# Chunked attention with a two-layer MLP behind it on one core: the opening stretch with and without 128 matmuls of the identity

## The chip, the cores and the metric

One core of one Trainium2 chip runs the whole program. The metric is the device time in microseconds (us) of one execution. A profiled execution also has a span, from the first to the last instruction of the program; all places in the profile (us) count from the start of that span.

## The reference

Attention is computed inside chunks of 64 tokens only, for 8 batches, 8 heads, 576 tokens and a head dimension of 64; its output, 4608 tokens by 512, goes through two matrix products with a leaky ReLU between them.

```python
# q, k, v: [8, 8, 576, 64]; w_in: [512, 2048]; w_out: [2048, 512]
scores = scale * np.matmul(q_c, k_c.transpose(0, 1, 2, 4, 3))   # chunks of 64
scores = scores - np.max(scores, axis=-1, keepdims=True)
attn = np.exp(scores)
attn = attn / (np.sum(attn, axis=-1, keepdims=True) + 1e-09)
out = np.matmul(attn, v_c)
x = out.transpose(0, 2, 1, 3).reshape(4608, 512)
h = x @ w_in
g = np.maximum(0.01 * h, h)
return g @ w_out
```

## The kernel before, in words

**Units and blocks.** The attention works on 36 units of 128 tokens (two chunks, all eight heads). The MLP works on blocks of 128, 256 or 512 tokens (`BLOCKS`, line 46). All matmuls are in 16 bits, but for the transposes of the first unit, whose q and k come in 32 bits by a DMA each from SyncE and ScalarE (lines 121 to 124).

**Stages of a unit u.** Each is a small function, and the text names it by its letter:
- `tq`, `tk` (line 259): four transposes of q, of k, on TensorE into PSUM (`qp`, `kp`, one buffer each).
- `q` (lines 272, 274): two copies of `qp` into the block-diagonal tile `QZ`, on ScalarE where the name ends in .1, else on VectorE. `k` (lines 279, 281): the copy of `kp` to `KT`.
- `s` (line 309): eight matmuls of 64 columns, the scores, into PSUM `Sp` (one buffer).
- `m`, `b` (VectorE, lines 318, 322): row maximum, and the difference. `x` (ScalarE, line 328): the exponential. `z` (VectorE, lines 334 to 338): sum, plus 1e-9, reciprocal. `n` (VectorE, line 343): the product.
- `e` (line 351): four transposes of the probabilities on TensorE into `tpe`; `c` (line 358 on ScalarE, 360 on VectorE): the copy to `et`.
- `v` (line 376): eight matmuls of 64 columns with the values (`VB`) into `xp`. `tpe` and `xp` share a single PSUM buffer (tag `ox`), so `e` of a unit waits until `a` of the unit before it is done.
- `a` (ScalarE, line 389): the copy of `xp` into `xT`, the MLP's input.

**The MLP.** `A j.a` (line 157) is one group of sixteen 128-column matmuls of the first layer for the 128-token block j, from quarter a of `w_in`; `G j.a` (line 172, ScalarE) its leaky ReLU. `B j.p` (line 182) is four 512-column matmuls of the second layer; `O j` (line 193) copies a finished block out, and a DMA stores it. The first-layer and second-layer results, and the tile of the filler, share four PSUM buffers (tag `mm`).

**What sets the order.** Every engine executes its instructions in program order. For the first six units that order is a string written out by hand, `FRONT` (line 430), which names the stages one after another; the loop from line 473 on follows for the other units. In `FRONT` stand also `y` (VectorE memsets of `QZ` and `VB`), `w` (the same on ScalarE), `I` (the identity copied to 32 bits on ScalarE, line 410, which the first `tq` and `tk` use), and `i` followed by a number: that many filler matmuls, `idle`. Their result is read by nobody:

```python
def idle(n):
    t = psp.tile([128, 4, 128], FP32, name="idle", tag="mm", bufs=4)
    for i in range(n):
        nc.tensor.matmul(out=t[:, i % 4, :], lhsT=ident, rhs=ident, start=True, stop=True)
```

`FRONT` calls it nine times: i12, i4, i23, i55, i7, i3, i3, i12 and i9, together 128 matmuls of 128 columns, each with its weight load. The nine calls are all in the part ahead of `A0.0`, the first group of the MLP.

**Loads.** GpSimd issues the DMAs of q, k, v and the weights in the order of `LOADS` (line 133); the identity is made there after the first of them (line 140).

Of the kernel before, what the change touches and what calls it, by code (L numbers as in the profile page):

```python
# [16 lines left out]
def kernel(  # L17
# [401 lines left out]
    def zero_act(i):  # L419
# [8 lines left out]
            )  # L428

    FRONT = (  # L430
        "y0 y1 y2 y4 w3 I y5 i12 tq0 tk0 q0.1.1 q0.0 tq1 k0.1 q1.0.1 i4 s0 tk1 m0 k1 b0 q1.1.1 i23 s1 x0 "
        "m1 b1 z0 x1 z1 i55 tq2 q2.0.1 n0 i7 tk2 k2 q2.1 i3 e0 n1 c0.1 s2 m2 i3 v0 a0 b2 i12 e1 x2 c1 i9 "
        "v1 z2 A0.0 a1 A1.0 n2 G0.0 e2 A0.1 c2 v2 tq3 a2 A1.1 q3.1 G0.1 q3.0 tk3 A2.0 G1.0 k3.1 G1.1 s3 "
        "A0.2 G2.0 m3 A1.2 b3 x3 A2.1 G0.2 z3 A0.3 G1.2 tq4 G2.1 n3 A1.3 G0.3 e3 G1.3 A2.2 c3 q4.0.1 v3 "
        "tk4 a3 A2.3 k4.1 q4.1 A3.1 y6 G2.3 G2.2 A3.0 G3.1 s4 A3.3 m4 A3.2 b4 G3.3 G3.0 B0.1 G3.2 B3.1 x4 "
# [104 lines left out]
```

## Time and profile before

| | us |
|---|---|
| device time, median of 3 runs | 294.11 (294.11 to 294.14) |
| device time of the profiled execution | 294.1 |
| its span | 292.3 |
| TensorE busy | 284.4 |
| VectorE busy | 182.7 |
| ScalarE busy | 152.5 |
| filler matmuls (line 396) | 9.6 busy, 128 instructions, from 3.8 to 18.1 |
| first matmul of the MLP (line 157) | at 18.57 |

The 1.8 us between the device time and the span lie outside the program's own instructions. In a timeline row the first number is the start, the second the time from the first instruction's start to the last one's end; matmuls are pipelined, so one of them is shown with 219 ns or more although a row of them starts one every 56 ns. In the chain of waits the second number is only the time by which a piece carried the chain on, so there the time of n matmuls divided by n is their pace.

### The profile page before, as it was taken

To read this page: it belongs to the slowest core of one execution; us is meant where nothing else is said; L and a number is where in the kernel's file an instruction comes from. 1 tells how busy PE (TensorE), PEld (TensorE's weight loads), DVE (VectorE), ACT (ScalarE), POOL (GpSimd) and SP (SyncE) were. 2 spreads that over 40 slices of the span, in tenths; PEclk is the share of its full clock that TensorE was granted. 3 is DMA by queue.
4 is the path that set the end of the run, shared out by engine and by line. 5 is a ranking of instruction groups with operands and counts; after the bars stand their busy time and mean duration, and the time that the engine had idled before them with its cause. 6 is when DMAs were issued, how large, how long until landed. Compare 5 with 4: busy or idle time off the path is not lost.

```text
span 292.3 us, 6210 instructions
## 1 busy us (share of the span) xinstructions
PE 284.4 (97%) x2556; PEld 181.8 (62%) x2556; DVE 182.7 (63%) x338; ACT 152.5 (52%) x270; POOL 119.4 (41%) x148
## 2 busy tenths in 40 slices
PE   4999999999999999999999999999999999999995
PEld 3989955878677766767676754444454444444444
DVE  5776536879899898888877888787777720000000
ACT  5457713756456545646454547733763387127511
POOL 8857547898509837920394379210000000000000
PEclk9999999999999999999999999999999999999999
DMA  9999999999999999999499999992111320120022
GB/s 131 162 193 194 202 157 184 168 144 146 127 126 61 148 147 135 139 132 99 66 135 138 105 85 148 94 137 90 56 23 31 112 69 0 38 88 21 0 74 72
DMA packets 192332, 32.00 MB, mean 109 GB/s; under 512 B 183472, under 2 KB 187824, under 8 KB 192304
## 3 DMA queue, kind: packets, MB, share of 16 engines
q0 software_dynamic: 170208, 18.10, 114.0%
q1 hardware_dynamic: 21056, 13.24, 19.4%
q8 instruction: 20, 0.33, 0.4%
q10 hardware_dynamic: 1040, 0.26, 0.4%
q14 instruction: 8, 0.07, 0.1%
HBM read 36.70 MB, written 9.44 MB: 158 GB/s over the span
## 4 chain that ended last, share of the span: by engine, by line
PE 97%; POOL 1%; ACT 1%; issue 1%; DVE 0%; POOLq 0%
PE hT L157 43%; PE oP L182 41%; PE Sp L309 3%; PE xp L376 3%; PE idle L396 3%; PE oP L203 1%; PE qp L259 1%; PE tpe L351 1%; PE kp L259 1%; POOL k_in L69 0%; DVE QZ L274 0%; ACT KT L281 0%; ACT QZ L272 0%; POOL q_in L69 0%; ACT osb L211 0%
## 5 line engine op out<-in xcount | busy, mean ns | idle before, releaser
L157 PE MATMUL hT<-xT,w_inT 128*128 128x128 f16 (+2 forms) x1152 | 134.3, 273 | 0.0
L182 PE MATMUL oP<-w_outT,gT 128*128 128x512 f16 x560 | 128.2, 379 | 0.0
L157 PEld LDWEIGHTS <-w_inT 128*128 128x128 f16 x1152 | 90.0, 98 | 32.7
L172 ACT ACTIVATE gT<-hT 128x512 f16<-128x512 f32 x144 | 83.8, 597 | 32.5 <-PE hT L157 32.3
L182 PEld LDWEIGHTS <-gT 128*128 128x128 f16 x560 | 52.3, 98 | 56.3
L193 ACT ACTIVATE osb<-oP 128x512 f32<-128x512 f32 x35 | 20.9, 596 | 64.6 <-PE oP L182 62.7
L87 POOL DMA_DIRECT2D q_d<-in_q_dram x48 | 38.7, 818 | 35.3 <-DVE QZ L291 31.6
L318 DVE TENSOR_REDUCE mx<-Sp 128x8 f32<-128x512 f32 x36 | 24.9, 691 | 31.0 <-PE Sp L309 30.8
L87 POOL DMA_DIRECT2D k_d<-in_k_dram x48 | 38.7, 817 | 2.1 <-DMA q_d<-in_q_dram 1.1
L291 DVE STREAM_TRANSPOSE QZ<-q_d 64x512 f16<-64x512 f16 (+1 forms) x60 | 38.2, 644 | 0.4
L389 ACT ACTIVATE xT<-xp 128x512 f16<-128x512 f32 x36 | 21.4, 594 | 20.6 <-PE xp L376 20.6
L96 POOL DMA_DIRECT2D VB<-in_v_dram x16 | 18.4, 1159 | 20.8 <-PE xp L376 20.5
L334 DVE TENSOR_REDUCE z<-ex 128x8 f32<-128x512 f16 x36 | 23.6, 654 | 4.7 <-ACT ex L328 4.6
L322 DVE TENSOR_TENSOR sh<-Sp,mx 128x512 f32<-128x512 f32 x36 | 24.9, 691 | 1.2
L343 DVE TENSOR_TENSOR en<-ex,zi 128x512 f16<-128x512 f16 x36 | 24.8, 690 | 1.2
L328 ACT ACTIVATE ex<-sh 128x512 f16<-128x512 f32 x36 | 22.6, 628 | 5.3 <-DVE sh L322 5.3
L299 DVE STREAM_TRANSPOSE KT<-k_d 128x512 f16<-128x512 f16 (+1 forms) x30 | 19.4, 654 | 0.8
L376 PEld LDWEIGHTS <-VB 128*128 128x128 f16 x288 | 13.1, 98 | 5.6
L309 PEld LDWEIGHTS <-QZ 128*128 128x128 f16 x288 | 13.2, 99 | 5.4 <-DVE QZ L274 0.2
L309 PE MATMUL Sp<-KT,QZ 128*128 128x64 f16 x288 | 14.5, 195 | 0.1
L376 PE MATMUL xp<-et,VB 128*128 128x64 f16 x288 | 14.3, 193 | 0.0
L396 PE MATMUL idle<-ident 128*128 128x128 f16 x128 | 9.6, 233 | 3.8 <-POOL ident masks.py:199 3.8
(42 smaller groups left out, 104.2 us busy)
## 6 DMA issues: line engine op xcount, KB each, us to landing
out_dram<-osb SPq DMA_DIRECT2D x35, 256.0 KB, 2.3
VB<-in_v_dram POOLq DMA_DIRECT2D x16, 288.0 KB, 6.0
q_d<-in_q_dram POOLq DMA_DIRECT2D x48, 72.0 KB, 6.0
k_d<-in_k_dram POOLq DMA_DIRECT2D x48, 72.0 KB, 5.3
w_inT<-in_moe_w_in_dram POOLq DMA_DIRECT2D x8, 256.0 KB, 9.2
w_outT<-in_moe_w_out_dram POOLq DMA_DIRECT2D x4, 512.0 KB, 9.5
q_in<-in_q_dram POOLq DMA_DIRECT2D x7, 128.0 KB, 9.7
k_in<-in_k_dram POOLq DMA_DIRECT2D x7, 128.0 KB, 9.0
```

The source lines that it names most:

```text
L87: nc.gpsimd.dma_start(out=t[p0:p0 + 32, m, :, :, :].rearrange("p h b d -> p (h b) d"), in_=src[b, h0:h0 + 2, :, dh * 32:dh * 32 + 32].rear ...
L157: nc.tensor.matmul(out=hT[:, i, :], lhsT=w_inT[:, t, fc * 128:(fc + 1) * 128], rhs=xT[:, t, r0:r0 + tb], start=(t == 0), stop=(t == NT - 1),)
L172: nc.scalar.activation(out=gT[j][:, nf * a:nf * a + nf, :], in_=HT.pop((j, a)), func=AFT.Prelu, bias=0.0, scale=1.0, alpha=0.01)
L182: nc.tensor.matmul(out=o, lhsT=gT[j][:, fc, ti * 128:(ti + 1) * 128], rhs=w_outT[:, fc, :], start=(n == 0 and fc == part * 4), stop=(n == ...
L291: nc.vector.transpose(out=qz[s * CH:(s + 1) * CH, :, e0:e0 + n, s, :], in_=qkd[b][0][s * CH:(s + 1) * CH, :, at:at + n * CH].rearrange("p ...
L309: nc.tensor.matmul(out=Sp[:, i, :], lhsT=qz[:, 2 * m + g, e, :, :], rhs=kt[:, 2 * m + g, e, :], start=True, stop=True)
L318: nc.vector.tensor_reduce(out=MX[u], in_=SP[u], axis=AXL.X, op=ALU.max)
L322: nc.vector.tensor_tensor(out=SH[u], in0=SP.pop(u), in1=MX.pop(u).unsqueeze(2).to_broadcast((128, 8, CH)), op=ALU.subtract)
L328: nc.scalar.activation(out=E[u], in_=SH.pop(u), func=AFT.Exp, bias=0.0, scale=SCL)
L334: nc.vector.tensor_reduce(out=z, in_=E[u], axis=AXL.X, op=ALU.add)
L343: nc.vector.tensor_tensor(out=E[u], in0=ex, in1=ZI.pop(u).unsqueeze(2).to_broadcast((128, 8, CH)), op=ALU.mult)
L376: nc.tensor.matmul(out=xp[:, t, e, :], lhsT=VB[b % NVB][:, t, c, :], rhs=et[:, t // 2, e, t % 2, :] if u < UD else et[:, t % 2, e, t // 2, :],
```

## The change

The nine `i` entries are taken out of `FRONT`. All other entries stand in the same order, and the loads, tiles and loops are the same. `idle` stays defined and is not called.

```diff
     FRONT = (
-        "y0 y1 y2 y4 w3 I y5 i12 tq0 tk0 q0.1.1 q0.0 tq1 k0.1 q1.0.1 i4 s0 tk1 m0 k1 b0 q1.1.1 i23 s1 x0 "
-        "m1 b1 z0 x1 z1 i55 tq2 q2.0.1 n0 i7 tk2 k2 q2.1 i3 e0 n1 c0.1 s2 m2 i3 v0 a0 b2 i12 e1 x2 c1 i9 "
+        "y0 y1 y2 y4 w3 I y5 tq0 tk0 q0.1.1 q0.0 tq1 k0.1 q1.0.1 s0 tk1 m0 k1 b0 q1.1.1 s1 x0 "
+        "m1 b1 z0 x1 z1 tq2 q2.0.1 n0 tk2 k2 q2.1 e0 n1 c0.1 s2 m2 v0 a0 b2 e1 x2 c1 "
         "v1 z2 A0.0 a1 A1.0 n2 G0.0 e2 A0.1 c2 v2 tq3 a2 A1.1 q3.1 G0.1 q3.0 tk3 A2.0 G1.0 k3.1 G1.1 s3 "
...
```

## The prediction

> **What bounds the kernel now.** I read the page first: busy times, the 40 slices, the shares of the chain, and the group of the filler.
>
> ```profile
> PE 284.4 (97%) x2556; PEld 181.8 (62%) x2556; DVE 182.7 (63%) x338; ACT 152.5 (52%) x270; POOL 119.4 (41%) x148
> PE   4999999999999999999999999999999999999995
> PEclk9999999999999999999999999999999999999999
> L396 PE MATMUL idle<-ident 128*128 128x128 f16 x128 | 9.6, 233 | 3.8 <-POOL ident masks.py:199 3.8
> ```
>
> TensorE is busy from the first slice to the last. The list of what TensorE waited for, asked from 18.6 us to the end, has no row, and the only hole that the single instructions show there is 0.17 us ahead of e2, the transposes at 20.52. So whatever moves the start of A0.0 (18.57), or slows TensorE behind it, moves the end by as much, less those 0.17 us. The page's chain gives the filler 2.8% of the span; whether that time can be had back is decided by what each run of filler stands in front of. The chain in order of time shows TensorE's pace too:
>
> ```profile
> 8.20 0.43 PE idle L396 x4
> 8.63 0.43 PE Sp L309 x8
> 9.06 0.43 PE kp L259 x4
> 9.48 1.39 PE idle L396 x23
> 10.87 0.31 PE Sp L309 x8
> 11.18 3.07 PE idle L396 x55
> ...
> 18.34 0.39 PE xp L376 x8
> 18.73 1.79 PE hT L157 x32
> ```
>
> Four filler matmuls take 0.43 us at 8.2 (107 ns each) and 55 take 3.07 us at 11.2 (55.8 each): the same instruction runs at half pace up to about 9.6 us, and at full pace from there. (23 at 55.8 would be 1.28 us, the row has 1.39: two were still slow.) The page's clock row and its windows say full clock even before that, so there I go by the pace. That the clock is also taken away, the stretches behind the last matmul (end 288.9) show; the columns are the length, the busy time of PE, PEld, DVE, ACT and POOL, the granted clock, the DMA share and GB/s:
>
> ```profile
> 289.50:292.80 3.30, 0.00 (x0) 0.00 (x0) 0.00 (x0) 0.00 (x0) 0.00 (x0) 1.00 0.12 40
> 292.90:294.30 1.40, 0.00 (x0) 0.00 (x0) 0.00 (x0) 0.00 (x0) 0.00 (x0) 0.50 0.00 0
> ```
>
> The clock held through 3.9 us without a matmul and was half by 4.0. Last the timeline of the chain's end, to see what the filler covers:
>
> ```profile
> 15.28 0.40 PE L351 MATMUL tpe<-ident,en 128*128 128x128 f16 x4
> 15.71 0.60 ACT L358 ACTIVATE et<-tpe 128x512 f16<-128x512 f16 x1
> 16.36 0.39 PE L376 MATMUL xp<-et,VB 128*128 128x64 f16 x8
> 16.79 0.60 ACT L389 ACTIVATE xT<-xp 128x512 f16<-128x512 f32 x1 [0.48 <-PE xp L376]
> 17.44 0.38 PE L351 MATMUL tpe<-ident,en 128*128 128x128 f16 x4
> 17.86 0.42 DVE L360 COPY et<-tpe 128x512 f16<-128x512 f16 x1
> 18.34 0.39 PE L376 MATMUL xp<-et,VB 128*128 128x64 f16 x8
> ```
>
> e0, c0, v0, a0, e1, c1, v1 follow each other at 0.04 to 0.06 us, each the moment that the one before has ended. They alternate between TensorE and another engine, and the filler (i3, i12, i9) lies in between.
>
> **The change, run by run.** i12 (3.80 to 5.05): tq0 starts at 5.11, and its 32-bit identity is ready at 5.05 (ScalarE, 4.76 + 0.29). Nothing gained. i4: k0 ends on VectorE at 8.165 and s0 could start 0.05 later, at 8.22; it starts at 8.42, behind i4. That is the one place where filler delays: **-0.20**. i23: s1 starts at 10.78, q1 on ScalarE ends at 10.72. Covered. i55 and i7: tq2 and tk2 could go at 12.17 and 13.28 (their loads land at 12.12 and 13.23) instead of 14.09 and 14.71. But their copies stand in program order behind x1 on ScalarE and behind n0 on VectorE, and e0 waits for n0 (end 15.22), which ends an unbroken VectorE run from m1 (11.22) on. Nothing gained. i3, i3, i12, i9: the chain just shown. The nine filler tiles also leave the four `mm` buffers; nothing waited for these in the front. The loads come by GpSimd, which waits for no filler; w_in's first quarter has landed at 16.22, the second at 18.95, both early enough.
>
> So with an unchanged clock the whole change is worth 0.20 us. The cost is the clock. Without filler TensorE has, after the unchanged tq0 and tk0 (5.11 to 7.08), tq1, s0 and tk1 between 7.62 and 9.08, then s1 at 10.6, tq2 at 12.2, tk2 at 13.3, e0 at 15.3, s2 at 15.8 and v0 at 16.6, each 0.2 to 0.45 us of issue. In before, 3.1 us of unbroken work (3.80 to 6.87) had not raised the clock, and it rose only after another 1.95 us (7.62 to 9.57). I take the slow clock to last through the front.
>
> (1) *The chain at the slow clock.* Per step, slow row minus fast row: s1 like s0, 0.64 for 0.41: +0.23. e0 like tk1 (0.61) for 0.40: +0.21. v0 like s0, 0.64 for 0.39: +0.25 and the same for e1, 0.61 for 0.38: +0.23. v1 up to the issue of A0.0, 0.45 (s0 to tk1, 8.42 to 8.87) for 0.23: +0.22. Together 1.14; s2 slows too but ends as n1 does on VectorE, at 16.4. With i4's -0.20 A0.0 starts **+0.94** later, at 19.5. Bounds: -0.20 if all is fast, +0.94 if all is slow; I take the latter, as the slow rows are nearest to work in short bursts.
>
> (2) *The dense run until the clock rises.* From 19.5 TensorE has unbroken work at 107 instead of 55.8 ns per 128 columns, so each slow us loses 0.48. How long it lasts no row shows for such a run; the nearest two are 1.95 us (from the end of the pause to the rise) and 5.77 (from the first matmul to the rise). That makes 0.93 to 2.75; between two ends that are equally far I take the middle, 3.86 us: **+1.84**.
>
> (3) *Given back.* The hole ahead of e2: **-0.17**. n2 ends 0.45 later (c1 holds VectorE), at 20.9; e2 is reached only at 22.9.
>
> Sum: 0.94 + 1.84 - 0.17 = +2.61. The profiled execution had 294.1, as the median; so **296.7**, a span of 294.9. With (2) at its ends: 295.8 to 297.6.
>
> The Trainium skill, "TensorE: Matmul & The Clock Gate", "What's actually happening", says that activity is judged in free-running windows of 3.413 us. This trace agrees: rise (9.57) to fall (between 292.8 and 292.9) is 83.0 of them. By that rule the window edges here are 9.57, 19.81 and 23.22, the dense run is slow for 3.7 us, and the sum is 296.6.
>
> **Rivals.** *A, the clock rises at 9.6 anyway and holds.* Place: tq1, s0 and tk1, 1.26 us of issue where before has 1.95 unbroken. If that suffices, or if the rise comes with time and not with work, and if the bursts behind it hold the clock, nothing is left but i4: 294.1 - 0.2 = 293.9, not slower. It decides from the rise alone, as no later pause (at most 1.7 us, tk2 to e0) comes near the 3.9 us that the clock survived at the end. Against it: the 3.1 us that were not enough. The same page ("Why this matters for your kernels") asks only that no pause exceeds some 3 us; that rule would give this rival's time, and no row of the front can test it. A rise at 9.6 that is lost again before 19 would give 296.5, and counts with the forecast.
>
> *B, the front's bursts count.* The clock is up at A0.0 or under 1.95 us after it: 294.1 + 0.94 - 0.17 + (0 to 0.93) = 294.9 to 295.8. For it: v0, e1, v1 come close together. Against: they are still mostly pauses.
>
> *C, it takes longer than 5.77 us*, because the dense run starts just after a stretch judged idle: beyond 297.6, 0.48 per us, to about 298.5 with two more. Against: nothing interrupts the run.
>
> *D, the chain's 2.8% is simply saved*: 294.1 - 8.2 = 285.9. Against it stands the whole run-by-run list.
>
> **How the numbers follow.** Forecast 0.70, A 0.10, B 0.08, C 0.10, D 0.02. The forecast's own range is 295.8 to 297.6; taking in nearly all of B and the nearer half of C, 295.0 to 298.0 holds 0.82. About 0.2% (0.6 us) is what a measurement of this kernel can tell from no change. Faster: D and a little more, 0.03. Same: A, 0.11. Slower: 0.86.
>
> **What would show it.** Tk1 at 8.66, s1 at 10.56 with 53 ns between its matmuls (29 refutes step 1), n0 at 14.6 as before, A0.0 at 19.5, first-layer matmuls 107 ns apart up to 21.5 to 25.3 and 56 from there, no wait of TensorE behind it, and the same distance from that rise to the end. The forecast is wrong if s1 and v0 run at 29 ns, or if some copy or DMA that now has slack turns up ahead of A0.0.

## The result and the profile after

The kernel without the filler takes 296.52 us in the median of 4 runs (295.95 to 297.52), the one with it 294.12 (294.11 to 294.14): ratio 1.0093, 95% interval 1.008 to 1.0106, so 2.4 us slower. The profiled execution took 296.64 us with a span of 294.8.

The page of the kernel after, the lines that answer to those of before:

```profile
PE 280.0 (95%) x2428; PEld 176.7 (60%) x2428; DVE 184.0 (62%) x338; ACT 152.4 (52%) x270; POOL 119.4 (40%) x148
PE   2479999999999999999999999999999999999995
PEclk9999999999999999999999999999999999999999
```

TensorE has 4.4 us less to do and ends 2.5 us later. The first two slices now show its pauses. The clock row is the same and shows nothing of what follows. The chain of waits of the kernel after, in order of time (start, how long the piece carried the chain, what):

```profile
10.52 0.62 PE Sp L309 x8
...
15.22 0.62 PE tpe L351 x4
...
15.86 0.61 ACT et L358
...
16.51 0.60 PE xp L376 x8
...
17.13 0.61 ACT xT L389
...
17.78 0.60 PE tpe L351 x4
...
18.40 0.44 DVE et L360
...
18.88 0.58 PE xp L376 x8
19.46 3.41 PE hT L157 x32
22.88 0.27 PE tpe L351 x4
23.15 0.39 PE hT L157 x7
```

Two things are to be seen. Each burst of TensorE in the alternating chain takes about 0.6 us, against 0.4 in before; the copies between them take what they took. And the first 32 matmuls of the MLP take 3.41 us, 107 ns each, where before has 1.79 us for 32; the seven behind e2 are at 56 again. The clock came up at about 22.9, in the middle of e2. A0.0 starts at 19.28 (18.57 in before).

The one new hole of TensorE behind that is ahead of e3. The timeline of the kernel after (start, length, engine, operation) leads back to an addition on VectorE:

```profile
28.17 2.33 POOL L96 DMA_DIRECT2D VB<-in_v_dram  x2
...
29.68 0.82 DVE L336 TENSOR_SCALAR ze<-z 128x8 f32<-128x8 f32 x1
...
30.45 0.93 POOL L69 DMA_DIRECT2D q_in<-in_q_dram  x1
...
31.52 0.23 PEld L351 LDWEIGHTS <-en 128*128 128x128 f16 x4 [0.26 <-DVE en L343]
```

The same addition in before:

```profile
27.44 0.20 DVE L336 TENSOR_SCALAR ze<-z 128x8 f32<-128x8 f32 x1
...
28.49 2.33 POOL L96 DMA_DIRECT2D VB<-in_v_dram  x2
```

The addition `ze` on eight numbers per row takes 0.82 us, where the median is 0.17. It stands beside GpSimd's issue of the loads of v; in before it fell ahead of these. n3 and e3 come later by that, and TensorE has a hole of 0.25 us. Why the addition takes longer there was not tried.

### The profile page after: what moved, and what is told of

Same layout as the page of the kernel before. It is cut to its first block, busy times and chain, and to the rows that moved or that the text cites. A ratio compares the mean times of both kernels' runs of the same rounds, so it can differ in the third digit from the quotient of the medians.

```text
span 294.8 us, 5955 instructions
## 1 busy us (share of the span) xinstructions
PE 280.0 (95%) x2428; PEld 176.7 (60%) x2428; DVE 184.0 (62%) x338; ACT 152.4 (52%) x270; POOL 119.4 (40%) x148
## 4 chain that ended last, share of the span: by engine, by line
PE 93%; DVE 3%; ACT 2%; issue 1%; ACTq 0%
PE hT L157 42%; PE oP L182 41%; PE xp L376 3%; PE Sp L309 3%; PE oP L203 1%; PE tpe L351 1%; PE qp L259 1%; DVE z L334 1%; PE kp L259 1%; DVE mx L318 0%; DVE sh L322 0%; ACT L127 0%; DVE en L343 0%; ACT QZ L272 0%; DVE ze L336 0%
## 5 line engine op out<-in xcount | busy, mean ns | idle before, releaser
L157 PE MATMUL hT<-xT,w_inT 128*128 128x128 f16 (+2 forms) x1152 | 135.9, 275 | 0.0
L157 PEld LDWEIGHTS <-w_inT 128*128 128x128 f16 x1152 | 91.6, 99 | 32.7
L389 ACT ACTIVATE xT<-xp 128x512 f16<-128x512 f32 x36 | 21.4, 594 | 22.5 <-PE xp L376 22.5
L299 DVE STREAM_TRANSPOSE KT<-k_d 128x512 f16<-128x512 f16 (+1 forms) x30 | 19.4, 654 | 0.8
L376 PE MATMUL xp<-et,VB 128*128 128x64 f16 x288 | 14.6, 195 | 0.7 <-DVE et L360 0.5
L336 DVE TENSOR_SCALAR ze<-z 128x8 f32<-128x8 f32 x36 | 10.9, 302 | 1.2
```

Source lines behind the costliest of these rows:

```text
L157: nc.tensor.matmul(out=hT[:, i, :], lhsT=w_inT[:, t, fc * 128:(fc + 1) * 128], rhs=xT[:, t, r0:r0 + tb], start=(t == 0), stop=(t == NT - 1),)
L376: nc.tensor.matmul(out=xp[:, t, e, :], lhsT=VB[b % NVB][:, t, c, :], rhs=et[:, t // 2, e, t % 2, :] if u < UD else et[:, t % 2, e, t // 2, :],
```

## The experiments

Three theories were held against each other. *Clock theory*, that of the prediction: the filler's only use is to get and keep TensorE's clock up. *Order theory*: it spaces the stages so that copies and loads do not collide. *Presence*: it is enough that TensorE has instructions at all. The quoted paragraph under each change is what was expected before that run. The kernel before ran again beside them: its median was 294.0 us in 23 runs (293.51 to 294.91) beside the 47 matmuls, the two columns, the first three runs of filler and the kernel without i4, and 293.81 in 21 runs (293.52 to 294.39) beside the other four.

**Order or clock: 47 matmuls in the pauses** (to the kernel after)

```diff
-"... z1 tq2 q2.0.1 n0 tk2 k2 q2.1 e0 ... m2 v0 a0 b2 e1 x2 c1 "
+"... z1 i7 tq2 q2.0.1 n0 i6 tk2 k2 q2.1 i17 e0 ... m2 i3 v0 a0 b2 i8 e1 x2 c1 i6 "
```

> The kernel after, with 47 filler matmuls put back in the pauses behind s1 alone (7 before tq2, 6 before tk2, 17 before e0, 3 before v0, 8 before e1, 6 before v1), each run short enough for its pause at the slow pace. Clock theory: the clock rises between 12.6 and 17, A0.0 starts at 18.6 to 19.1, nothing is slow behind it: 294.1 to 294.8. Order theory: the spacing is not that of before; 295 to 296.5.

Measured: 294.24 us in the median of 10 runs, nine of them from 294.08 to 294.47 and one 295.52; ratio to before 1.001 (0.9997 to 1.0022). Two rows of its chain:

```profile
10.52 0.62 PE Sp L309 x8
...
20.56 0.40 PE tpe L351 x4
```

s1 is still slow, and the clock is up from 13.4. A0.0 starts at 18.55 and e2 at 20.56 (before: 18.57 and 20.52). tq2 and tk2 stand as early as in the kernel after, and a third of the filler, elsewhere, gives back all but some tenths of a us. The order theory falls.

**Presence or work: fillers of two columns** (to before)

```diff
-nc.tensor.matmul(out=t[:, i % 4, :], lhsT=ident, rhs=ident, start=True, stop=True)
+nc.tensor.matmul(out=t[:2, i % 4, :2], lhsT=ident[:, :2], rhs=ident[:, :2], start=True, stop=True)
```

> All 128 filler matmuls stay where they are, but with two weight columns and two moving columns each in place of 128. Clock theory with the array's work as what counts: the clock rises only in the dense run, 296.0 to 297.5 as after. If it is enough that instructions keep arriving at TensorE, the clock rises at 9.6 and the time is 293.9 to 294.2.

Measured: 296.82 us (296.07 to 297.4, 4 runs); ratio 1.009 (1.0068 to 1.0111), the same as without any filler. Its chain:

```profile
10.63 0.62 PE Sp L309 x8
...
19.59 2.71 PE hT L157 x32
```

s1 is slow, and 32 matmuls in 2.71 us are 18 slow ones and 14 fast (18 x 106.7 + 14 x 55.8 ns): the clock came up at 21.4, in the dense run. Presence falls; what counts is how much passes through the array, not the number of instructions.

**Does a risen clock hold?** (to before: only i12, i4 and i23 stay)

```diff
-"m1 b1 z0 x1 z1 i55 tq2 q2.0.1 n0 i7 tk2 k2 q2.1 i3 e0 n1 c0.1 s2 m2 i3 v0 a0 b2 i12 e1 x2 c1 i9 "
+"m1 b1 z0 x1 z1 tq2 q2.0.1 n0 tk2 k2 q2.1 e0 n1 c0.1 s2 m2 v0 a0 b2 e1 x2 c1 "
```

> i12, i4 and i23 stay, the six runs behind s1 go. The clock rises as before at 9.6; the question is whether the short bursts of the front hold it. Clock theory if it holds through pauses under 3 us (the longest is some 2 us, tk2 to e0): 294.1. Clock theory if bursts of 0.2 us do not hold it: it falls between 13.0 and 16.4, and the time is 295.5 to 297, with first-layer matmuls 107 ns apart from A0.0 on. Order theory: 296.5, as after, with 56 ns at A0.0.

Measured: 296.52 us (296.09 to 296.88, 4 runs); ratio 1.0085 (1.0063 to 1.0107). This profile has the fall in its clock column. Stretches of 3.41 us of it, the length named in the prediction, laid so that the changes of the clock fall on their edges (length, busy time of PE, PEld, DVE, ACT, POOL, granted clock, DMA share, GB/s):

```profile
8.58:11.99 3.41, 2.22 (x44) 1.95 (x41) 2.41 (x4) 2.06 (x4) 2.54 (x4) 1.00 2.23 147
11.99:15.40 3.41, 1.19 (x12) 0.68 (x12) 3.23 (x9) 1.82 (x3) 2.40 (x4) 1.00 1.29 197
15.40:18.82 3.42, 2.16 (x28) 1.77 (x29) 2.93 (x5) 1.82 (x3) 1.64 (x3) 0.50 1.74 181
18.82:22.23 3.41, 3.41 (x36) 3.41 (x34) 1.25 (x4) 1.19 (x2) 2.29 (x4) 0.50 1.33 203
```

The clock was up from 8.58, held through the first stretch, and was taken away behind the second, in which TensorE had twelve transposes: 12 x 55.8 ns, 20% of it. It came back after a full stretch. The chain has the same at its pace:

```profile
10.50 0.41 PE Sp L309 x8
...
15.45 0.61 PE Sp L309 x8
...
19.03 3.38 PE hT L157 x32
```

No pause was longer than 1.8 us (s1 done at 10.91, tq2 at 12.75). A rule on the length of a pause alone does not fit: behind the last matmul of the ten profiles the clock still held for 3.5 to 5.2 us without any.

**Where the level lies: with i55, without the five runs behind it** (to before)

```diff
-"... i55 tq2 q2.0.1 n0 i7 tk2 k2 q2.1 i3 e0 n1 c0.1 s2 m2 i3 v0 a0 b2 i12 e1 x2 c1 i9 "
+"... i55 tq2 q2.0.1 n0 tk2 k2 q2.1 e0 n1 c0.1 s2 m2 v0 a0 b2 e1 x2 c1 "
```

> i12, i4, i23 and i55 stay; the five short runs behind tq2 go (34 matmuls). In the run with three runs of filler the clock was lost after a stretch of 3.4 us in which TensorE had 20% of work. Here each such stretch up to A0.0 has 45% or more. Clock theory with a level between 20% and 45%: the clock holds, 294.0 us. If the level is higher: it falls at 16 to 20, and the time is 295 to 297.

Measured: 294.83 us in the median of 10 runs; ratio 1.0036 (1.0016 to 1.0056). Four runs lie at 294.02 to 294.12, five at 294.66 to 295.22, one at 297.15. The profiled one (294.12) kept its clock, with 45% of work in its emptiest stretch, the second of these (by the columns of its matmuls; the busy time in the row also counts the time that each takes to pass through):

```profile
12.48:15.89 3.41, 2.77 (x50) 2.42 (x48) 3.21 (x10) 2.02 (x4) 1.64 (x3) 1.00 1.20 193
15.89:19.31 3.42, 2.00 (x40) 1.69 (x37) 2.99 (x6) 2.10 (x4) 1.74 (x3) 1.00 1.81 180
```

The other six have no profile, but each run's mean granted clock is on record. It is 1.000 in the four at 294.1, 0.994 in the five and 0.992 in the last. One stretch of 3.41 us at half clock takes 0.006 off the mean, so the clock was taken away in these six, in the five for about one stretch. So neither answer alone: the last 34 fillers are not needed in some runs and are in others. An estimate from the single matmuls of the profiled run suggests why: if the stretches lay otherwise against the same front, the emptiest one ahead of A0.0 would hold anything from 26% to some 55%. In the front of before no place of a stretch behind the rise gives less than 70%. That their place decides is argued, not shown.

**i4, the run that stood in the way** (to before)

```diff
-"... q1.0.1 i4 s0 ..."
+"... q1.0.1 s0 ..."
```

> Only i4, the one run of filler that stood in the way of a stage, is left out. Clock theory: s0 0.20 us earlier, the clock still rises by 9.7, everything behind as in before: 293.9 us. If the four matmuls are needed for the rise (they are 0.43 us of the work in the 3.4 us ahead of it), it comes up to 3.4 us later and the time is 294.5 to 296. Order theory (the filler only spaces the stages): 293.9.

Measured: 294.37 us in the median of 12 runs; ratio 1.0021 (0.9999 to 1.0043), inconclusive as a mean, since the runs fall into two groups: six from 293.54 to 293.85, six from 294.88 to 296.61. The upper six are where the second expectation put them, one above its range. The lower six are where the first one did, but ten of the 23 runs of before lie at 293.85 or less as well, so they show no gain. The chain of the profiled one, the longest:

```profile
9.22 2.45 PE idle L396 x23
11.68 0.43 PE Sp L309 x8
12.10 3.69 PE idle L396 x55
15.80 0.24 PE qp L259 x4
```

s0 came 0.21 us earlier (8.21 us), as expected. But the clock stayed down until about 13.3, so 23 fillers took 2.45 us in place of 1.39 and held s1 back, and the 55 took 3.69 in place of 3.07. Filler that is sized for the fast clock becomes the bound at the slow one. A0.0 starts 1.44 us later than in before, and the end is 2.5 later: the rest are holes behind A0.0, the largest 0.6 us at 83.6, where v waits for the DMA of `et`.

**The spread of the kernel after**, once more with no edit.

> The kernel after once more, for the spread of its runs. Clock theory with judging windows that lie anywhere against the start of the program: A0.0 again at 19.3, the rise anywhere between 21.5 and 25.3, and the time 296.64 plus 0.48 us for each us that the rise lies behind 22.9; all runs between 295.9 and 297.6. Fixed windows: the rise at 22.5 to 23.2 each time.

Measured: 296.08 us (295.9 to 296.91, 4 runs); ratio 1.0079 (1.0062 to 1.0096); the profiled run 296.12. Its chain:

```profile
19.47 2.98 PE hT L157 x32
22.45 0.22 PE tpe L351 x4
```

A0.0 starts at 19.29, as before. 32 matmuls in 2.98 us are 23 slow and 9 fast: the clock rose at 21.9, 1.0 us earlier than in the other profile, and the time is 0.52 us less. At 0.48 per us the rise makes 0.48 of that. A0.0 started at the same time in both, so neither a fixed time in the program nor a fixed length of dense work makes the rise.

**Filler in front of ready work** (to the kernel after)

```diff
-"v1 z2 A0.0 ..."
+"v1 z2 i32 A0.0 ..."
```

> The kernel after with 32 filler matmuls in one place, between v1 and A0.0, where TensorE has work to do. Clock theory: they run at 107 ns, hold A0.0 back by 3.4 us to 22.7, and the work behind is fast at once: 296.6 + 3.4 - 1.7 = 298.3 us. So filler in front of ready work costs more than the slow clock does. If the slow run were not what the time is lost to, 300.

Measured: 299.22 us (298.12 to 299.54, 4 runs); ratio 1.0173 (1.0153 to 1.0194). The profiled run is the lowest:

```profile
19.49 2.74 PE idle L396 x32
22.22 1.79 PE hT L157 x32
```

The filler waited out the slow time, and the MLP was fast at once. Against before the end came 4.02 us later: A0.0 had been held back by 3.5 us, less the 0.17 of e2 and plus a wait of v for the DMA of `et` at 85 us, which set the matmuls back by 0.70 (0.5 in the list of waits). The median decides nothing, as it lies between the two expectations, 298.3 and 300; the row of the MLP does, 56 ns a matmul from its first one on. The forecast was 0.9 us too low: I had left out that wait, and took the rise to come by the end of the filler, which the other three runs may not have had; no profile shows them. That the filler cost more than the slow clock does is clear: all four runs lie above all eight of the kernel after.

**A version to beat both** (to before; `f` is filler of a zeroed tile, 38 matmuls)

```diff
+    blank = sbp.tile([128, 128], FP16, name="blank")
+    nc.vector.memset(blank, 0.0)
...
+            nc.tensor.matmul(out=t[:, i % 4, :], lhsT=blank, rhs=blank, start=True, stop=True)
...
-"... y5 i12 tq0 tk0 q0.1.1 q0.0 tq1 k0.1 q1.0.1 i4 s0 ..."
+"... y5 f38 tq0 tk0 q0.1.1 q0.0 i5 tq1 k0.1 q1.0.1 s0 ..."
```

> A version meant to beat both: 38 filler matmuls of a zeroed tile from 1 us on in place of i12 (which starts at 3.8), no i4, five fillers ahead of tq1 where TensorE pauses for 0.5 us, the rest as before. Clock theory: the clock is up at 3.5 to 7, before the stages of the first unit, so tk1 and s0 come 0.5 to 1.1 us earlier and the whole behind them: 292.9 to 293.6. If zeroed operands do not count as work, or if the time of the early stages is set by the loads alone: 294 or more.

Measured: 293.40 us (293.11 to 293.84, 11 runs); ratio to before 0.9982 (0.9973 to 0.9991). Its chain (line numbers are two to seven higher here):

```profile
1.05 4.18 PE idle L403 x38
5.23 0.54 PE qp L261 x4
...
8.15 0.22 PE kp L261 x4
8.37 1.28 PE idle L398 x23
...
17.69 1.79 PE hT L159 x32
```

tk1 is fast (0.22 for 0.43), all of the 23 fillers are, and A0.0 starts at 17.53, 1.04 us ahead of before. The filler of zeros raised the clock. The version is faster than both kernels, by 0.18% against before. In the medians that is 0.4 us and not 1.0: the profiled run is the shortest of the eleven, and the profiled run of before, at 294.1, is longer than the median of those beside it. Three things were changed at once, and which of them gave the gain is not separated.

## Why the prediction was right, step by step

**What bounds it.** Right. Behind A0.0 the time goes as TensorE's issue goes. The sum of the measured terms, 0.71 + 1.71 - 0.17 + 0.25 = 2.50, stands against a span longer by 2.51 us (294.83 to 292.32). That 296.7 comes so near to the 296.64 of the profiled run and the median of 296.52 is in part luck: the first two terms were 0.36 us too large together, and 0.25 of that was made up by a hole that the prediction did not have.

**Run by run.** Right: i4 alone delayed a stage. tq0 starts at 5.10, s0 at 8.21 (forecast 8.22), s1 at 10.52 (10.56), n0 at 14.52 (14.6). tq2 and tk2 went at 11.8 and 12.9, and nothing came of it, as said.

**(1) The slow chain: +0.94 forecast, +0.71 measured.** The mechanism holds at each link, the size is off. s1 starts 0.26 us earlier (0.20 forecast); then, from a stage's start to the start of what it releases, s1 loses 0.20, e0 0.21, v0 0.19, e1 0.20 and v1 0.17 (forecast 0.23, 0.21, 0.25, 0.23 and 0.22). The slow rows that I took, s0 and tk1 of before, stood behind unbroken work, and in them the second matmul starts 73 and 88 ns behind the first; in the bursts behind a pause it is 28 to 49 ns for s1, v0 and v1, and 79 and 59 for e0 and e1.

**(2) The slow dense run: +1.84 forecast, +1.71 measured.** It lasted 3.58 us for 3.86 forecast. That the middle between the two rows came so near is luck: it was 2.6 us in the second profile of the same kernel. What the rows supported was the range of 1.95 to 5.77, and both lie in it. The price of 0.48 per us is confirmed by that pair. The edges named ahead of the result (19.81 and 23.22) were carried over from the run of before; in these two runs the rise came at 22.86 and 21.85.

**(3) Given back: -0.17, right**, and a term that I had not looked for, +0.25 ahead of e3: delay does not only add slack, it also moves a stage beside another engine's work.

**Rivals.** A did not occur: in neither profile of the kernel after did the clock rise ahead of 21.8. Its reasoning was wrong, too: it was said to decide from the rise alone, as no pause came near 3.9 us. The run with the first three fillers shows a clock that rose, and was lost with no pause over 1.8 us. The Trainium skill, "TensorE: Matmul & The Clock Gate", "Why this matters for your kernels", asks for pauses under some 3 us; this run kept to that and lost the clock all the same, behind a stretch of 3.41 us with 20% of work. The windows of that page of the Trainium skill ("What's actually happening") do agree: rise to fall is 6.83 us there, two of them, and in the other nine profiles it is a whole number of them too, 80 to 84. B did not occur (the chain's bursts made 45% of a stretch and did not raise the clock), C neither. D fell at once: TensorE has 4.4 us less to do and it ends later.

What stays open is the exact level of work. An estimate: count what the columns of the single matmuls take in each stretch of 3.41 us (107 ns for 128 columns at the slow pace and 56 at the fast, 213 for a 32-bit transpose at the slow one), with a matmul that lies across an edge split there. Over all ten profiles up to 75% of work did not raise the clock (both stretches ahead of the late rise in the run without i4), and every stretch from 77% did. To hold it, 45% was enough and 20% was not. By this count a stretch laid anywhere ahead of s1 in the kernel after holds at most some 74%: rival A missed its rise by little.

## What to carry to other kernels

An instruction whose result nobody reads can be worth its place: count it as free only where it stands in a wait, and ask what pace TensorE has without it. Read the pace from matmuls of one shape (time of n by n), not from a mean clock on the page. Where the pace depends on when the clock rises, a kernel has a spread of its own: compare many runs, and size filler so that it fits its pause at the slow pace as well.

## What was not expected of the hardware

- The clock is lost to thin work, not only to a pause: 20% of work in 3.41 us, pauses of 1.8 us at most.
- Transposes count as work. In the run with the first three fillers the clock rose behind 5.16 to 8.58 us, where all but 0.58 us of TensorE's work was transposes; 1.1 us of other matmuls with 0.4 of transposes, in the kernel after at 16.0 to 19.4, did not raise it.
- Matmuls of zeros raise the clock like others (38 of them, the transposes at 5.2 are fast).
- An addition on 128 by 8 numbers on VectorE took 0.82 us beside GpSimd's issue of DMAs, for 0.17 in the median. In all ten profiles none without GpSimd's work beside it took more than 0.17, and all that took over 0.3 stood beside an issue of DMAs. Not every one beside an issue is long, though: in the run without i4 the one at 29.1 us stands beside the loads of v and took 0.17. This was seen, not tried.
